# Two query chunks in turn per head group, an earlier x load, later use of GpSimd results, and more zero products in a gated mix of two attentions

## The chip, the cores and the metric

The kernel runs on one core of a Trainium2 chip, in one launch. A NeuronCore has five engines that run their own instruction queues and wait for each other by semaphores: TensorE (PE in the profile; its weight loads are PEld), VectorE (DVE), ScalarE (ACT), GpSimd (POOL) and SyncE (SP), which here only issues DMAs. The metric is the device time of one execution in microseconds, lower is better.

## The reference

Two attentions over the same input `x` (1 x 2048 x 512, bf16, 32 heads of 16), mixed by a gate for each row:

```python
g = _sigmoid((x * gate_w).sum(-1, keepdims=True))
a = _A_ref(x, A_wqkv, A_wo)        # full attention: softmax(q k^T / 4) v, then @ wo
b = _B_ref(x, B_wqkv, B_wo)        # each query sees 8 keys: positions s, s-2, ..., s-14
return g * a + (1 - g) * b
```

Part A needs 32 x 2048 x 2048 exponentials, and part B 32 x 2048 x 8.

## The kernel before

**Part A.** Queries are cut into four chunks of 512 (`QW`), heads into eight groups of four (`NG`). A pair of a chunk and a group is a period (`periods`, 32 of them, chunk by chunk: all eight groups of chunk 0, then of chunk 1, and so on). In a period the scores are made in units: 128 keys of one head against 512 queries, 64 units a period. A unit is one matmul into a slot of a PSUM ring (`qk`, tiles `ring`), one exponential (`ex`, on ScalarE, tiles `pT`) and one matmul with the values (`pv`, into `acc`). Units are taken in sets of three and two by turns, one ScalarE instruction for a set (`sets`); the ring for three and the ring for two have one buffer each. A few units of each period (`n_dve`) take another way: VectorE makes their exponential by a polynomial on the bits (`d_group`, tiles `dt`, `dg`, `pd`), so that ScalarE has fewer.

For each head group K is projected once for all 2048 keys (`k_proj`, four steps of 512 keys into `kt_all`, with a copy `kc` and a maximum `km` on VectorE; `selk` makes a scale `rowq` of the four maxima). Q is projected for each period (`q_proj`: matmuls, a mask `mg`, a scaled copy `ev` into `qt`). V is projected in blocks of heads (`v_proj`). The doubled Q and K weights `wtw` are made by `twice`, two copies each for heads 0 to 3 and for the rest. `x` comes in four tiles (`load_x`), is transposed on TensorE into PSUM (`pxt`) and copied to `xT`, half by ScalarE and half by VectorE. `warm` gives TensorE matmuls on ones before data is there.

At a period's end VectorE transposes and divides the accumulator (`po1`, `po2`, `po3`, tiles `accT`, `ott`, `oat`). When a chunk has all groups, its four row tiles are multiplied with `wo` (`a_part`, `b_part`) and leave (`dout`). For the last chunk the first three quarters of that product are made ahead, kept in the space of `kt_all`, and the rest is added at the end (`tail`).

**Part B.** For each of 16 row tiles (`b_tile`): K and V projections to a scratch in DRAM (`kv_scr`), two DMAs that bring the eight shifted neighbours (`ksh`, `vsh`), products and sums on GpSimd (`logits_half`, `av_half`, tiles `prod`, `lg`, `ob`, `obb`), a softmax in between on VectorE and ScalarE, then 16 transposes on TensorE (`fin`) and a copy on VectorE (`oe`, tile `obt`).

**The order.** No engine's order is written out by hand. Each step is an `op` with an engine, a cost, a due time `dl`, an earliest time `rel`, steps it needs (`deps`) and buffers it takes or uses (`tok`). `list_schedule` plays these on a clock of its own, engine by engine, and takes among what can start the step that is due first; `slack` adds time to a result before TensorE is thought to have it. The instructions are then issued in that order, chained on each engine, so an engine that waits for one instruction holds all behind it.

`list_schedule` also adds zero products: matmuls of zeros onto an accumulator that is in use, which change nothing in it. Where the work of the last 3.41 us (`SPAN`) falls short of a share `cover` and the list shows TensorE idle, it fills the idle time; where the lack is above `force` products, it adds one without idle time:

```python
if lack - o.zeros * ZERO > CFG["force"] * ZERO and recent and not (o.rows and rows):
    o.zeros += 1
    late = ZERO
```

The helper lines L247 (all but TensorE) and L256 (TensorE) record nearly every operation, so the profile's groups are told apart by tiles.

Of the kernel before, what the change touches and what calls it, by code (L numbers as in the profile page):

```python
# [19 lines left out]
    n_dve=(2,) * 4 + (3,) * 4 + (5,) * 18 + (6,) * 5 + (5,),  # L20
# [4 lines left out]
    force=9.0,  # L25
# [11 lines left out]
    v_slack=0.3,  # L37
    unit=0.457,
    t0=22.0,
# [5 lines left out]
H = 32  # L45
# [30 lines left out]
class Op:  # L76

    def __init__(self, eng, occ, fn, dl, deps=(), alloc=(), use=(), lat=None, rel=0.0, name="",
                 after=(), rows=False, cover=None, slack=None):
        self.eng, self.occ, self.fn, self.dl, self.rel, self.name = eng, occ, fn, dl, rel, name  # L80
        self.rows, self.zeros = rows, 0
        self.slack = (CFG["v_slack"] if eng == "dve" else 0.0) if slack is None else slack
        self.cover = cover if cover is not None else (occ if not callable(occ) else 0.0)
        self.after = [d for d in after if d is not None]
        self.deps, self.alloc = [d for d in deps if d is not None], list(alloc)
        self.lat = (occ if not callable(occ) else occ(0.0)) + LAT[eng] if lat is None else lat
        self.done = None
        for tk in list(alloc) + list(use):
            tk.ops.append(self)
# [9 lines left out]
def list_schedule(ops):  # L99
# [29 lines left out]
    while len(out) < len(ops):  # L129
# [49 lines left out]
        for s_ in succ.get(o, ()):  # L179
            left[s_] -= 1  # L180
            if left[s_] == 0:
                s_.ready = max([s_.rel] + [d.end if d.eng == s_.eng else d.done + (d.slack if s_.eng == "pe" else 0.0)
                                           for d in s_.deps]
                               + [d.t for d in s_.after])
                cand[s_.eng].append(s_)
# [4 lines left out]
def kernel(  # L190
# [94 lines left out]
    periods = [(c_, i) for c_ in range(NC) for i in range(NG)]  # L285
    NP = len(periods)
    dorder = [(t, j) for t in range(NT - 1, NT - 1 - NTD, -1) for j in range(4)]
# [31 lines left out]
    rowc = const.tile([128, 2], FP32, name="rowc")  # L319
# [3 lines left out]
    xT = const.tile([128, DC, S], BF16, name="xT")  # L323
# [11 lines left out]
    def init_dve():  # L335
        V.memset(ones_t[:], 1.0)
        V.memset(rowc[:, 0:1], 0.0)
        V.memset(rowc[:, 1:2], 1.0)
        V.memset(rowl[:], LIFT / DH)
        V.memset(magn[:], 0x7FFFFFFF)  # L340
        for j in range(4):
            V.memset(rowc[32 * j:32 * j + DH, 0:1], 1.0)
            V.memset(rowc[32 * j:32 * j + DH, 1:2], 0.0)
            V.memset(rowl[32 * j:32 * j + DH, :], 0.0)
            V.memset(magn[32 * j:32 * j + DH, :], 0xFFFFFFFF)
        V.memset(z32[:], 0.0)
        V.memset(ott2[:], 0.0)
# [10 lines left out]
    o_id = op("pool", 1.2, init_pool, -9.0)  # L358
    o_init_p = op("pool", 2.8, init_pool2, -8.0, deps=[o_id])
# [24 lines left out]
    def twice(part, h0, h1):  # L384
        def s():
            for r in range(2):
                V.tensor_copy(out=wtw[:, :, part, h0:h1, r, :],
                              in_=wraw["t"][:, part * DC:(part + 1) * DC, h0 * DH:h1 * DH].rearrange("p c (h d) -> p c h d", d=DH))
        return s
# [17 lines left out]
    o_x[0] = op("sp", 0.5, load_x(0), -9.0, alloc=[xtok[0]], lat=5.5)  # L407
    wtok = tok("vsh", 1)
    o_wk = op("sp", 0.5, load_w(1), -8.9, alloc=[wtok], lat=6.5)
    o_x[1] = op("sp", 0.5, load_x(1), -8.8, alloc=[xtok[1]], lat=7.5)  # L410
    o_x[2] = op("sp", 0.5, load_x(2), -8.7, alloc=[xtok[2]], lat=9.5)
    o_wq = op("sp", 0.5, load_w(0), -8.6, use=[wtok], lat=11.0)
    o_x[3] = op("sp", 0.5, load_x(3), -8.5, alloc=[xtok[3]], lat=12.0)
    o_wv = op("sp", 0.5, load_w(2), -8.4, lat=13.0)
    o_two = {}
    for part, o_ld, dl0 in ((1, o_wk, -6.0), (0, o_wq, -5.0)):
        o_two[part, 0] = op("dve", 0.4, twice(part, 0, 4), dl0, deps=[o_ld], use=[wtok])
        o_two[part, 1] = op("dve", 1.2, twice(part, 4, H), 4.0 - part, deps=[o_ld], use=[wtok])
# [4 lines left out]
    def warm():  # L423
        t_ = misc_ps([128, QW])
        for _ in range(3):
            mm_ct(t_, ones_t[:, 0:128], ones_t[:], True, True)
    o_warm = op("pe", 4.0, warm, -9.0, deps=[o_init_d], alloc=[tok("misc", 2)])

    o_xt = []
    for sc in range(NC):  # L430
# [13 lines left out]
        def ev(half, sc=sc, st=st):  # L444
            def s():
                dst = xT[:, 2 * half:2 * half + 2, sc * QW:(sc + 1) * QW]
                src = st["p"][:, 2 * half:2 * half + 2, :]
                if half == 0:
                    A.copy(out=dst, in_=src)
                else:  # L450
                    V.tensor_copy(out=dst, in_=src)
# [20 lines left out]
    o_selk = {}  # L472

    def k_proj(i, sc, tag, dl, rel=0.0):
# [3 lines left out]
        def part(c0, c1):  # L478
            def s():
                if c0 == 0:  # L480
                    st["pk"] = misc_ps([128, QW], tag=tag)
                for c in range(c0, c1):
                    mm_heads(st["pk"], c, 1, i, xT[:, c, sc * QW:(sc + 1) * QW], c == 0, c == DC - 1)
            return s

        def kc():
            V.tensor_scalar(out=kt_all[:, i, sc * QW:(sc + 1) * QW], in0=st["pk"][:], scalar1=rowc[:, 0:1],
# [6 lines left out]
        c = op("dve", 0.71, kc, dl - 0.8, deps=[b], use=[tk])  # L494
        return op("dve", 0.70, km, dl, deps=[b, c], use=[tk])

    def selk(i, dl):
        def s():
            V.tensor_reduce(out=kmax[:, i:i + 1], in_=kmax_all[:, i, :], axis=AX.X, op=ALU.max)
            V.scalar_tensor_tensor(out=rowq[:, i:i + 1], in0=kmax[:, i:i + 1], scalar=rowc[:, 1:2], in1=rowc[:, 0:1],  # L500
                                   op0=ALU.mult, op1=ALU.subtract)
            V.tensor_scalar(out=rowq[:, i:i + 1], in0=rowq[:, i:i + 1], scalar1=-1.0, scalar2=None, op0=ALU.mult)
        o_selk[i] = op("dve", 0.32, s, dl, deps=o_kc[i])

    for i in range(NG):
        o_kc[i] = []
        for sc in range(NC):
            if i == 0:
                o_kc[i].append(k_proj(i, sc, ("misc", "acc", "misc", "misc")[sc], -2.0 + sc))
            else:  # L510
                o_kc[i].append(k_proj(i, sc, "misc", S0[i] - 7.0 - 4.5 * (NC - 1 - sc), rel=S0[i - 1] - 6.0 if i > 1 else 10.0))
        selk(i, 2.0 if i == 0 else S0[i] - 6.0)
# [4 lines left out]
    def v_proj(h0, h1, tb, TB, tag, dl, rel=0.0):  # L517
# [4 lines left out]
        def mk(half):  # L522
            def s():
                if half == 0:
                    st["pv"] = misc_ps([128, TB, n], tag=tag)
                for tt in range(half * TB // 2, (half + 1) * TB // 2):
                    t = tb + tt
                    for c in range(DC):
                        mm(st["pv"][:, tt, :], xT[:, c, t * 128:(t + 1) * 128],
# [14 lines left out]
    v_proj(0, 4, 0, 8, "misc", 3.0)  # L544
    v_proj(0, 4, 8, 8, "misc", 4.0)
    for h0, h1, pn in ((4, 8, 1), (8, 16, 2), (16, 24, 4), (24, 32, 6)):
        TB = 512 // ((h1 - h0) * DH)
        for tb in range(0, NT, TB):
            late = tb + TB > NT - NTD
            v_proj(h0, h1, tb, TB, "misc", S0[pn] + (4.0 if late else 1.0 + tb * 1.3), rel=max(22.0, S0[pn - 1] - 4.0))  # L550


    def shift(pi):
        return cfg["shift"] if pi > NG else 0.0
# [3 lines left out]
    def q_proj(pi, tag, dl, rel=0.0):  # L558
# [6 lines left out]
        def part(c0, c1):  # L565
            def s():
# [3 lines left out]
                for c in range(c0, c1):  # L570
                    mm_heads(st["p1"], c, 0, i, xT[:, c, c_ * QW:(c_ + 1) * QW], c == 0, c == DC - 1)
# [9 lines left out]
        seq = steps(part, tk, dl - 4.0, [o_two[0, min(i, 1)], o_init_d] + o_xt[c_] + ([o_selk[i]] if pi else [o_kc[0][1]]),  # L581
# [5 lines left out]
    q_proj(0, "acc", 2.5)  # L587
# [5 lines left out]
    for sc in range(NC):  # L593
# [3 lines left out]
        def zc(sc=sc, st=st):  # L597
            st["p"] = misc_ps([1, QW])
            for c in range(DC):
                mm(st["p"][0:1, :], gw[:, c:c + 1], xT[:, c, sc * QW:(sc + 1) * QW], c == 0, c == DC - 1, tile_position=(0, 0))  # L600
# [9 lines left out]
        a = op("pe", 0.9, zc, dl, deps=[o_bw] + o_xt[sc], alloc=[tk], rel=22.0)  # L610
# [31 lines left out]
    def b_tile(t):  # L642
# [5 lines left out]
        def proj(key, off):  # L648
          def part(c0, c1):
            def s():  # L650
# [6 lines left out]
                for c in range(c0, c1):  # L657
                    mm_ct(st[key], xT[:, c, t * 128:(t + 1) * 128], bw[:, c, off * D:(off + 1) * D], c == 0, c == DC - 1)
# [169 lines left out]
    for k, us in enumerate(sets):  # L828
# [18 lines left out]
        kd = [o_kc[periods[pi][1]][t // TPC] for pi, t, j in us]  # L847
# [36 lines left out]
    def d_group(pi, gr, lo, hi):  # L884
# [44 lines left out]
        for q_, (t, j) in enumerate(gr):  # L929
            tx = tok("misc", 2)  # L930
            a = op("pe", 0.20, dq(q_), hi - 7.5 + q_, rows=True, deps=[o_q[pi], o_kc[i][t // TPC]], after=[prev or d_last[0]], alloc=[tx], use=[q_tok[pi]],
# [19 lines left out]
    for pi, (c_, i) in enumerate(periods):  # L951
# [4 lines left out]
        if i % 2 == 0:  # L956
            ott_tok[pi // 2] = tok("ott", 2)
        to = ott_tok[pi // 2]
# [6 lines left out]
        def po2(pi=pi, st=st):  # L965
# [3 lines left out]
            g0 = DH * (pi % 2)  # L969
            V.tensor_tensor(out=ott2[:, pi // 2 % 2, :, g0:g0 + DH], in0=st["a"][:, :, 0:DH], in1=rd_bc, op=ALU.mult)  # L970

        def po3(pi=pi, c_=c_, i=i):
            if c_ not in oat_tiles:
                oat_tiles[c_] = work.tile([128, NG // 2, QW], BF16, name="oat", tag="oat", bufs=2)
            V.transpose(out=oat_tiles[c_][:, i // 2, :], in_=ott2[:, pi // 2 % 2].rearrange("p b d -> p (b d)"))
        a = op("dve", 0.75, po1, E - 1.0, deps=o_pv[pi], alloc=[ta], use=[acc_tok[pi]], slack=cfg["a_slack"])
        o_ott[pi] = op("dve", 0.90, po2, E + 4.0, deps=[a], alloc=[to] if i % 2 == 0 else [], use=[ta] + ([to] if i % 2 else []))
        if i % 2:
            o_oat[pi] = op("dve", 0.74, po3, E + 6.0, deps=[o_ott[pi], o_ott[pi - 1]] + ([o_oat[pi - 2]] if pi > 1 else []),
# [6 lines left out]
    for t in range(NT):  # L986
        c_, tt = t // TPC, t % TPC
        st = {}
        last = c_ == NC - 1
        ng = NG // 2 - 1 if last else NG // 2  # L990
        E = S0[NG * c_ + 2 * ng]
        dl = E + (4.0 + 4.0 * tt if last else 10.0 + 14.0 * tt)
# [9 lines left out]
        def a_ev(st=st, t=t, tt=tt, last=last):  # L1002
            if last:
                st["fa"] = fa_view(tt)
# [25 lines left out]
        for k0 in range(0, ng, STEP):  # L1030
            k1 = min(ng, k0 + STEP)
            a = op("pe", WAVE(k1 - k0), a_part(k0, k1), dl - 4.0 + 0.3 * k0,
                   deps=[a, o_oat[NG * c_ + 2 * ng - 1], o_g, o_wo] if k0 == 0 else [a],
# [8 lines left out]
        else:  # L1042
            a = op("dve", 0.71, b_ev, dl, deps=[a, fe], use=[tk])
            tag = ("misc", "acc", "misc", "rA")[tt]
            otag = ("osb", "osb", "kvs", "kvs")[tt]
            tk, tos = tok(tag, 2 if tag == "misc" else 1), tok(otag, 2)
            E2 = S0[NP]
# [9 lines left out]
            b = op("pe", 0.26, tail, E2 + tt, deps=[o_oat[NP - 1]], alloc=[tk], use=[oat_tok[c_]])  # L1057
# [40 lines left out]
```

## Time and profile before

| | |
|---|---|
| median of the runs | 967.3 us (962.67, 967.30, 967.45) |
| profiled execution | 969.36 us, span 967.6 us |
| mean granted TensorE clock | 0.902 |
| busy: PE, DVE, ACT, POOL | 830.3, 788.3, 882.3, 741.9 us |
| exponentials of sets (ACT, `pT` from `ring`) | 761, 873.8 us |
| DMA | 47.34 MB, mean 49 GB/s |

The page gives the busy time of each engine, then the span in 40 slices: each digit is the busy share in tenths, and PEclk is the TensorE clock that was granted, in tenths of full speed. The views of waits name the engine that waited, the tile it was about to write, and what ended the wait, with the total in us, the number of times and the longest. In a timeline a row has its start, its busy time, engine, line, operation, output and input, and in brackets the idle time before it with what ended that. A view of stretches gives, for each stretch, its length, the busy time and count of PE, PEld, DVE, ACT and POOL, the granted clock, the DMA share and GB/s.

### The profile page before, as it was taken

To read this page: it belongs to the slowest core of one execution; us is meant where nothing else is said; L and a number is where in the kernel's file an instruction comes from. 1 tells how busy PE (TensorE), PEld (TensorE's weight loads), DVE (VectorE), ACT (ScalarE), POOL (GpSimd) and SP (SyncE) were. 2 spreads that over 40 slices of the span, in tenths; PEclk is the share of its full clock that TensorE was granted. 3 is DMA by queue.
4 is the path that set the end of the run, shared out by engine and by line. 5 is a ranking of instruction groups with operands and counts; after the bars stand their busy time and mean duration, and the time that the engine had idled before them with its cause. 6 is when DMAs were issued, how large, how long until landed. Compare 5 with 4: busy or idle time off the path is not lost. (4 is left out here: it accounts for less than half of the span.)

```text
span 967.6 us, 18043 instructions
## 1 busy us (share of the span) xinstructions
PE 830.3 (86%) x7361; PEld 253.5 (26%) x7361; DVE 788.3 (81%) x915; ACT 882.3 (91%) x783; POOL 741.9 (77%) x539
## 2 busy tenths in 40 slices
PE   6999989989898887788888888999798897789985
PEld 3333333232222222222222222222212222221221
DVE  5477769878879999879989989889987898988641
ACT  2799999999989998899999989899989999989996
POOL 1369688795999999999999999999999996700000
PEclk9999999899989998877898989679968979986898
DMA  8302030201311111111110311110211010000000
GB/s 262 101 2 99 1 100 1 87 12 56 99 66 56 55 56 44 55 44 46 54 49 13 104 55 54 46 44 31 69 55 50 12 50 2 1 1 1 1 1 22
DMA packets 43995, 47.34 MB, mean 49 GB/s; under 512 B 1876, under 2 KB 41348, under 8 KB 43912
## 3 DMA queue, kind: packets, MB, share of 16 engines
q1 hardware_dynamic: 43912, 46.19, 15.1%
q8 instruction: 57, 0.93, 0.4%
q14 instruction: 26, 0.21, 0.1%
HBM read 39.86 MB, written 6.33 MB: 48 GB/s over the span
## 5 line engine op out<-in xcount | busy, mean ns | idle before, releaser
L247 ACT ACTIVATE pT<-ring 128x1536 bf16<-128x1536 f32 x761 | 873.8, 1308 | 60.4 <-PE ring L256 57.4
L256 PE MATMUL ring<-qt,kt_all 32*128 32x512 bf16 x1903 | 325.5, 412 | 97.1 <-ACT pT L247 92.5
L247 POOL TENSOR_TENSOR prod<-prod 128x512 f32<-128x512 f32 (+1 forms) x208 | 314.0, 1522 | 6.3
L256 PE MATMUL acc<-pT,vp_all 128*17 128x512 bf16 (+1 forms) x1903 | 256.9, 420 | 2.2 <-DVE accT L247 1.3
L256 PEld LDWEIGHTS <-kt_all 32*128 32x128 bf16 x2048 | 104.7, 92 | 424.9 <-issue 420.3
L247 POOL TENSOR_TENSOR prod<-vsh,lg 128x512 f32<-128x512 bf16 x128 | 178.1, 1421 | 48.9 <-issue 37.8
L247 POOL TENSOR_TENSOR prod<-ksh,qb 128x512 f32<-128x512 bf16 x128 | 173.6, 1385 | 38.9 <-DMA ksh<-kv_scr 36.5
L247 DVE SCALAR_TENSOR_TENSOR dg<-dt,dg 128x1024 bf16<-128x1024 uint16 (+1 forms) x84 | 144.9, 1725 | 2.3
L247 DVE TENSOR_SCALAR dt<-misc 128x512 f32<-128x512 f32 x145 | 98.6, 687 | 50.0 <-PE misc L256 33.6
L247 DVE SCALAR_TENSOR_TENSOR pd<-dg,dt 128x1024 uint16<-128x1024 bf16 (+1 forms) x84 | 136.8, 1629 | 2.2
L247 DVE SCALAR_TENSOR_TENSOR dg<-dt 128x1024 bf16<-128x1024 uint16 (+1 forms) x84 | 121.9, 1451 | 2.7
L256 PE MATMUL acc<-ones_t,z 128*32 128x512 bf16 x292 | 110.4, 420 | 0.0
L256 PE MATMUL misc_ps<-xT,wtw 128*32 128x512 bf16 x1024 | 92.4, 419 | 3.3 <-DVE kmax_all L247 3.1
L256 PEld LDWEIGHTS <-vp_all 128*17 128x17 bf16 (+1 forms) x2048 | 48.6, 89 | 124.6 <-issue 118.6
L256 PE MATMUL misc<-qt,kt_all 32*128 32x512 bf16 x145 | 61.2, 426 | 9.0 <-DVE kvs L247 3.4
L256 PE MATMUL misc_ps<-bw,xT 128*32 128x512 bf16 x768 | 68.0, 395 | 1.1 <-DVE dt L247 0.9
L247 DVE STREAM_TRANSPOSE accT<-acc 128x512 f32<-128x512 f32 x32 | 22.7, 709 | 34.5 <-PE acc L256 34.3
L256 PEld LDWEIGHTS <-xT 128*32 128x32 bf16 (+1 forms) x1088 | 35.5, 98 | 34.3 <-issue 24.5
L256 PE MATMUL acc<-pd,vp_all 128*17 128x512 bf16 x145 | 40.3, 435 | 0.8 <-DVE pd L247 0.8
L256 PEld LDWEIGHTS <-z 128*32 128x32 bf16 x292 | 27.9, 98 | 40.1 <-issue 29.8
L256 PEld LDWEIGHTS <-wtw 128*32 128x32 bf16 x1024 | 26.4, 100 | 39.0 <-issue 22.7
L247 DVE TENSOR_SCALAR kt_all<-misc_ps,rowc 128x512 bf16<-128x512 f32 x32 | 25.7, 804 | 11.9 <-PE misc_ps L256 11.7
(68 smaller groups left out, 468.1 us busy)
## 6 DMA issues: line engine op xcount, KB each, us to landing
ksh<-kv_scr SPq DMA_DIRECT2D x16, 1024.0 KB, 6.0
vsh<-kv_scr SPq DMA_DIRECT2D x16, 1024.0 KB, 5.5
kv_scr<-kvs SPq DMA_DIRECT2D x16, 256.0 KB, 2.1
xld<-in_A_x_dram SPq DMA_DIRECT2D x4, 512.0 KB, 8.0
out_dram<-osb SPq DMA_DIRECT2D x16, 128.0 KB, 1.7
bw<-in_B_wqkv_dram SPq DMA_DIRECT2D x1, 1536.0 KB
wraw<-in_A_wqkv_dram SPq DMA_DIRECT2D x2, 512.0 KB, 8.2
wv<-in_A_wqkv_dram SPq DMA_DIRECT2D x1, 512.0 KB, 9.0
```

What stands on the lines that cost most here:

```text
L247: return chain_on(key, f(*a, **k))
L256: return chain(nc.tensor.matmul(out, lhsT=lhsT, rhs=rhs, start=start, stop=stop, **kw))
```

## The change

The periods run over pairs of chunks: group 0 of chunk 0, group 0 of chunk 1, group 1 of chunk 0, and so on, then the same for chunks 2 and 3. Each head group's K and V are therefore first needed two periods after those of the group ahead, and two chunks end together. Both of the last two chunks now have their product made ahead in part. `n_dve` is given anew (142 units for VectorE, before 145).

The fourth tile of `x` is loaded ahead of the Q weights; `xT` is two tiles, one for each copying engine; the K copies of group 0 go to ScalarE; the doubled weights, but for the K weights of heads 0 to 3, are made by GpSimd; `warm` has 32 matmuls and not 12; the first V projections and the K projections of group 1 come after the start; `rowq` needs one instruction less.

In the list a result of GpSimd counts 4 us later for any engine that takes it up (`g_slack`), and `force` goes from 9 to 1. The start of the exponentials that the due times are reckoned from (`t0`) goes from 22.0 to 18.5.

```diff
-    n_dve=(2,) * 4 + (3,) * 4 + (5,) * 18 + (6,) * 5 + (5,),
+    n_dve=(3,) * 2 + (4,) * 14 + (5,) * 16,
-    force=9.0,
+    force=1.0,
+    g_slack=4.0,
-    t0=22.0,
+    t0=18.5,
...
-        self.slack = (CFG["v_slack"] if eng == "dve" else 0.0) if slack is None else slack
+        self.slack = {"dve": CFG["v_slack"], "pool": CFG["g_slack"]}.get(eng, 0.0) if slack is None else slack
...
-                s_.ready = max([s_.rel] + [d.end if d.eng == s_.eng else d.done + (d.slack if s_.eng == "pe" else 0.0)
+                s_.ready = max([s_.rel] + [d.end if d.eng == s_.eng else d.done + (d.slack if s_.eng == "pe" or d.eng == "pool" else 0.0)
...
-    periods = [(c_, i) for c_ in range(NC) for i in range(NG)]
+    periods = [(2 * cp + s, i) for cp in range(NC // 2) for i in range(NG) for s in range(2)]
...
-    xT = const.tile([128, DC, S], BF16, name="xT")
+    xTs = [const.tile([128, 2, S], BF16, name=f"xT{h}") for h in range(2)]
...
+            E_ = V if part == 1 and h0 == 0 else G
             for r in range(2):
-                V.tensor_copy(out=wtw[:, :, part, h0:h1, r, :],
+                E_.tensor_copy(out=wtw[:, :, part, h0:h1, r, :],
...
-    o_wq = op("sp", 0.5, load_w(0), -8.6, use=[wtok], lat=11.0)
-    o_x[3] = op("sp", 0.5, load_x(3), -8.5, alloc=[xtok[3]], lat=12.0)
+    o_x[3] = op("sp", 0.5, load_x(3), -8.6, alloc=[xtok[3]], lat=9.2)
+    o_wq = op("sp", 0.5, load_w(0), -8.5, use=[wtok], lat=10.2)
...
-        for _ in range(3):
+        for _ in range(8):
             mm_ct(t_, ones_t[:, 0:128], ones_t[:], True, True)
...
         def kc():
+            if i == 0:
+                A.activation(out=kt_all[:, i, sc * QW:(sc + 1) * QW], in_=st["pk"][:], func=ACT.Identity, scale=rowc[:, 0:1],
+                             bias=rowc[:, 1:2])
+                return
...
-                o_kc[i].append(k_proj(i, sc, "misc", S0[i] - 7.0 - 4.5 * (NC - 1 - sc), rel=S0[i - 1] - 6.0 if i > 1 else 10.0))
-        selk(i, 2.0 if i == 0 else S0[i] - 6.0)
+                o_kc[i].append(k_proj(i, sc, "misc", S0[2 * i] - 16.0 - 9.0 * (NC - 1 - sc), rel=max(T0 + 1.0, S0[2 * i] - 60.0)))
+        selk(i, 2.0 if i == 0 else S0[2 * i] - 15.0)
...
-    v_proj(0, 4, 0, 8, "misc", 3.0)
-    v_proj(0, 4, 8, 8, "misc", 4.0)
-    for h0, h1, pn in ((4, 8, 1), (8, 16, 2), (16, 24, 4), (24, 32, 6)):
+    v_proj(0, 4, 0, 8, "acc", T0 + 2.0, rel=T0 - 2.0)
+    v_proj(0, 4, 8, 8, "misc", T0 + 3.0, rel=T0 - 2.0)
+    for h0, h1, pn in ((4, 8, 2), (8, 16, 4), (16, 24, 8), (24, 32, 12)):
...
-        last = c_ == NC - 1
+        last = c_ >= NC - 2
```

## The prediction

> **What bounds the kernel now.** I read the page first, for which engine has no spare time, then the waits, then stretches of the trace with their granted clock, then single moments. The page:
>
> ```profile
> PE 830.3 (86%) x7361; PEld 253.5 (26%) x7361; DVE 788.3 (81%) x915; ACT 882.3 (91%) x783; POOL 741.9 (77%) x539
> ...
> ACT  2799999999989998899999989899989999989996
> ...
> PEclk9999999899989998877898989679968979986898
> ```
>
> ScalarE is full from the third of the 40 slices to the end. Its work is 761 exponentials, one per set, and no edit makes one cheaper. So the time is: the start up to the first exponential, 761 sets, what delays a set, and the tail. The waits say what delays one (us in total, times, longest):
>
> ```profile
> PE ring L256 <- ACT pT L247: 92.5, 281, 1.3
> ACT pT L247 <- PE ring L256: 57.4, 76, 9.4
> ...
> POOL prod L247 <- DMA ksh<-kv_scr: 36.5, 1, 36.5
> ...
> PE misc_ps L789 <- POOL obb L247: 4.3, 1, 4.3
> ```
>
> ScalarE waits 57.4 us for scores; 9.4 of them lie before the first exponential, 48 later. Where those 48 fall is seen in stretches (length, busy time and count by engine, clock, DMA):
>
> ```profile
> 30.00:176.00 146.00, 134.39 (x1448) 47.37 (x1440) 104.88 (x156) 143.39 (x130) 105.83 (x87) 1.00 0.18 55
> 273.00:367.00 94.00, 79.60 (x765) 25.44 (x758) 88.15 (x92) 93.23 (x84) 92.20 (x64) 1.00 0.19 59
> 405.30:422.40 17.10, 13.98 (x81) 2.79 (x83) 10.48 (x12) 11.22 (x10) 16.63 (x13) 0.50 0.19 62
> 879.80:896.80 17.00, 17.00 (x78) 2.73 (x76) 11.94 (x13) 14.95 (x14) 0.00 (x0) 0.50 0.00 1
> ```
>
> At full clock ScalarE is 98 to 99% busy; at half clock 66 and 88%. The trace holds 21 half-clock stretches after the start, 181 us together, each a multiple of 3.41 us. I cut the full-clock time into windows of 3.41 us and counted how long the array streamed in each (a 512-column pass as 0.213 us): all 16 windows under 45% were followed by half clock, 5 of 39 between 45 and 55%, none of 159 above. So thin TensorE work, not only standing still, brings the half clock here.
>
> Last, the start and one stall:
>
> ```profile
> 1.89 2.13 POOL L247 MEMSET vp_all<- 128x480 bf16 x1
> ...
> 11.09 0.69 DVE L247 COPY xT<-pxt 128x1024 bf16<-128x1024 bf16 x1 [2.32 <-ACT xT L247]
> ...
> 27.03 0.81 DVE L247 TENSOR_SCALAR qt<-misc_ps,rowq,rowl 128x512 bf16<-128x512 f32 x1
> ...
> 28.33 3.90 ACT L247 ACTIVATE pT<-ring 128x1536 bf16<-128x1536 f32 x3 [9.40 <-PE ring L256]
> ```
>
> ```profile
> 408.42 0.62 PE L789 MATMUL misc_ps<-ident,obb 128*32 128x128 bf16 x16 [4.28 <-POOL obb L247]
> ...
> 409.68 1.02 ACT L247 ACTIVATE pT<-ring 128x1024 bf16<-128x1024 f32 x1 [3.72 <-PE ring L256]
> ```
>
> ScalarE starts at 28.33, behind VectorE, which works almost without a gap from 14.4 to 27.8. And TensorE once stood 4.28 us before the transposes of a GpSimd result, score matmuls queued behind them; ScalarE lost 3.72.
>
> **The start.** From 14.36 on VectorE's row holds, before the first exponential, five K copies (0.80 each, 4.0), two copies of doubled weights (0.35 and 1.15) and one reduce for head group 1 (0.68) that are gone from there in the new order, and one small rowq step (0.15): 6.3 us, which gives 22.0. The other way is the new chain. One 512 KB load lands every 1.5 us (transposes released at 5.11 and 8.12, the K weight copy at 6.59), so x tile 3 lands near 11.1 instead of 12.6 and the Q weights near 12.6 instead of 11.1. From there: transposes 1.07 per tile, ScalarE's x copy 1.01, VectorE's 0.69 still behind it (the order keeps that wait), the reduce 0.68, ScalarE's K copy behind the reduce (512 columns: between 0.55, half the 1.01 of 1024, and VectorE's 0.80), K matmuls 1.05 per half, the mask 0.75, maxima and rowq 0.4, qt 0.81, scores 0.4: 20.0 with TensorE at full clock from 6 us, 22.5 when it stays at half to 12.7 as before (32 K matmuls took 3.27 there, against 1.05 for 16 later). The 32 warming matmuls instead of 12 decide that; they end near 4.9, before x lands at 5.1, so they cost nothing. I take 21.0: **-7.3** (-5.8 to -8.3). What had been done before the start now stands between the first score matmuls: half of the V projection (64 matmuls took 2.73, so 1.4), K matmuls of group 1 and B projections. Covered, it costs nothing; uncovered up to 3.5; **+1.5**, about the V half, since only two score rings are ahead there.
>
> **GpSimd copies of weights.** Two copies of 256 columns, then four of 1792, no row of which is on GpSimd. Nearest rows: the plain memset 0.55 for 544 (1.0 ns a column), the products 1.42 for 512 (2.8), the strided memset 2.13 for 480 (4.4). TensorE's first K matmul of group 1 stands behind set 3 and waits for the second large copy; behind it on TensorE are all later scores. The Q weights land at 12.6; the K copies are done at 16.7, 24.0 or 30.8 by the three prices, and TensorE is there at about 24.4. Cost 0, 0 or 6.4; I take 0, by the products, which read bf16 with the same inner runs of 16. GpSimd's own first product waited for ksh until about 38, so it loses nothing.
>
> **Head groups in turn.** Units on ScalarE rise from 1903 to 1906, so at 28.33 to 958.8 for 1903, 0.49 each: **+1.4** for three. VectorE loses three units of 0.69 and 2.8 (its dg and pd rows, 403.6 us for 145), 10 us, off the path. The rest is where K and V projections stand: spread over sixteen periods, not eight. I counted TensorE's 512-column passes between score matmuls, per set, in sixths of the sets. Before: 3.86, 3.69, 3.27, 3.40, 3.41, 3.33, with half clock for 0, 12, 41, 55, 44, 27 us (the stretches' clocks). After: 3.68, 3.57, 3.65, 3.50, 3.31, 3.52. Read off the first pairs, that is some 13, 27, 17, 34, 40, 32 us: 163 instead of 181. A half-clock microsecond costs between 0.10 (half-clock stretches against 1.15 us a set at full clock, the stalled one corrected) and 0.30 (all 55 us by which 761 sets exceed 1.15 each, over 181). 18 at 0.14: **-2.5** (0 to -5.4).
>
> **GpSimd results later.** The order puts the sixteen transpose groups behind sets 71, 120, ... 334 (tile 6), ... 692. At 1.22 us a set from 21.0 each stands 14 us or more behind the time when GpSimd finished that tile before (tile 6: 428 against 408.4). The stall goes: **-3.7** (0 if GpSimd, which itself waits longer for softmax, slips as far; it ended at 842, so its slip alone costs nothing). Next late there is the score ring itself, 0.2 us.
>
> **Zero products everywhere.** 316 instead of 292; 43 of the new ones the list puts where it shows no idle stretch. At 0.213 that is 9.2 us put ahead of ready matmuls; TensorE waited 92.5 us for ScalarE's rings, which covers most. 0 to 9.2, taken at a quarter, since TensorE streams two thirds of full-clock time: **+2.0**.
>
> **Outputs and queues.** Two chunks' outputs come together, as many matmuls and copies as before, 0. On SP x tile 3 passes the Q weights (counted), and eight output DMAs stand last instead of four, four of them due a period earlier. Tail, 958.8 to 967.6, unchanged: 0, at worst +2.3 (the four last issues took 2.31).
>
> Sum: -7.3 + 1.5 + 1.4 - 2.5 - 3.7 + 2.0 = -8.6. The profiled execution took 969.4 with a span of 967.6; it becomes 960.8. The median of the runs is 967.3, so 958.7.
>
> **Rivals.**
> *Half clock spreads (slower).* The first 300 us are nearly free of it now, and exactly they get thinner; single windows decide, not means: stretches of three sets in which TensorE's work fills under half the time number 0 in sets 52 to 102 before and 9 after. Against: over the whole order they fall from 84 to 76. If the first two sixths become like the third (41 each) and the rest stays, half clock grows by 70 instead of shrinking: at 0.20, the middle of the two prices, 958.7 + 2.5 + 14 = 975. It decides from some 55 us of growth, where 972.1 is reached.
>
> *The GpSimd copies hold TensorE.* At 4.4 ns a column: 958.7 + 6.4 = 965. For: GpSimd's strided row. Against: its products. [...]
>
> *The zero products buy nothing.* If only standing still dropped the clock, the 43 would be pure TensorE time: 958.7 + 2.5 + 7.2 = 968. Against it stand the 21 falls: the longest TensorE stop after the start is 4.28 us, and the falls follow thin windows. [...]
>
> *The clock mostly holds.* If zero products and evenness cut half clock to 60 us, 121 at 0.20 go: 958.7 + 2.5 - 24 = 937. Against: the passes per set stay under 3.6 in four sixths.
>
> **How the numbers follow.** Forecast 0.54, half clock spreads 0.13, copies 0.14, zero products 0.07, clock holds 0.12. A measurement of this kernel tells about 0.5% from no change, so the borders are 962.5 and 972.1. The forecast's bounds add up to 951 at the good end and, halfway to all the bad ends, to 967; a quarter of it lies above 962.5. Faster: 0.40 + 0.12 + part of the copies' case, 0.10: 0.62. Slower: 0.13 and 0.03 from the forecast's worst sums: 0.16. Same: 0.22. The range leaves out half of the last rival and of the first: 943 to 975.
>
> **What would show it.** Right: first exponential at 20 to 22.5; no wait of TensorE for a GpSimd result above 1 us; half clock 140 to 185 us, more of it before 330 us and less behind; 763 exponentials of the same durations; tail near 8.8. Wrong: TensorE waiting for the doubled weights near 25 us; the clock of the first two stretches under 0.93; sets at full clock slower than 1.15 us, which would be the forced zero products.

## The result, and the profile after

| | before | after |
|---|---|---|
| median of the runs | 967.06 us (960.29 to 972.00) | 960.77 us (954.15 to 967.79) |
| profiled execution, its span | 969.36, 967.6 us | 963.95, 961.8 us |
| granted TensorE clock there | 0.902 | 0.917 |
| first exponential, last one's end | 28.33, 958.8 us | 21.57, 953.0 us |
| stretch between them (the row) | 930.5 us | 931.4 us |
| half clock in the row | 181 us in 21 falls | 154 us in 20 falls |
| tail | 8.8 us | 8.8 us |

Both medians are of 20 runs, taken beside each other. The ratio after to before is 0.9927, 95% interval 0.9906 to 0.9948: faster by 0.7%, 6.3 us in the medians and 5.4 us in the profiled pair. Of the 5.4, the start gives 6.8 and the row takes 0.9 back; 0.4 is time outside the profiled span. In the table of experiments the medians, the ratios and the means of half clock leave out six executions, of e3, e4, e6 and e7, that lay over 1.5% above their kernel's fastest.

The page of the kernel after, busy times and two rows of the 40 slices:

```profile
PE 828.1 (86%) x7405; PEld 254.6 (26%) x7405; DVE 769.1 (80%) x887; ACT 886.2 (92%) x789; POOL 750.9 (78%) x545
...
ACT  4899999999998899999988989979999999999995
...
PEclk9998999999998799989977989978999898999677
```

ScalarE now works from the end of the first slice on, and is still the full engine. Of the clock's slices 14 are below 9, where 18 were; the first of them is the fourth now (the eighth before), and the last three are low.

The waits (us in total, times, longest):

```profile
PE ring L257 <- ACT pT L248: 96.1, 287, 1.0
...
ACT pT L248 <- PE ring L257: 53.0, 73, 2.6
...
POOL prod L248 <- DMA ksh<-kv_scr: 21.4, 1, 21.4
...
POOL wtw L248 <- DMA wraw<-in_A_wqkv_dram: 8.9, 1, 8.9
```

ScalarE waited 57.4 us for scores before and waits 53.0 now. But 9.4 of the 57.4 lay ahead of the first exponential and 1.7 of the 53.0 do: inside the row it went from 48.0 to 51.3. All of ScalarE's idle time in the row, whatever the reason, is the same in both executions, 53.5 us: the row is 0.9 us longer because ScalarE works 0.9 us more in it. No wait of TensorE for GpSimd's `obb` is left in this view (4.3 us before). GpSimd's first products wait 21.4 us for `ksh`, not 36.5, behind the weight copies that it now makes first.

Two stretches (length, busy time and count by engine, clock, DMA share, GB/s):

```profile
30.00:176.00 146.00, 127.68 (x1273) 41.98 (x1265) 109.64 (x142) 140.41 (x127) 107.54 (x81) 0.96 0.17 53
313.80:324.00 10.20, 9.92 (x72) 2.09 (x70) 7.03 (x8) 7.55 (x7) 9.89 (x10) 0.50 0.01 2
```

The first is the same 146 us that ran at clock 1.00 with ScalarE busy 143.39 before. It has three windows of half clock now, and ScalarE is busy 140.41. The second is one of the half-clock stretches: ScalarE 7.55 of 10.20, 74%, as before between 66 and 88%.

The start, in the timeline:

```profile
10.88 0.78 ACT L248 ACTIVATE kt_all<-misc_ps,rowc 128x512 bf16<-128x512 f32 x1 [0.70 <-DVE kmax_all L248]
...
12.99 7.24 POOL L248 COPY wtw<-wraw 128x256 bf16<-128x256 bf16 x6 [8.94 <-DMA wraw<-in_A_wqkv_dram]
...
19.28 0.95 DVE L248 SCALAR_TENSOR_TENSOR rowq<-kmax,rowc 128x1 f32<-128x1 f32 x1
20.27 0.81 DVE L248 TENSOR_SCALAR qt<-misc_ps,rowq,rowl 128x512 bf16<-128x512 f32 x1
...
21.57 3.71 ACT L248 ACTIVATE pT<-ring 128x1536 bf16<-128x1536 f32 x3 [1.70 <-PE ring L257]
```

K copies on ScalarE take 0.78 us. The six weight copies of GpSimd, 7680 columns, take 7.24 us, 0.94 ns a column. `qt` is made at 20.27, not 27.03, and the exponentials begin at 21.57.

### The profile page after: what moved, and what is told of

It is laid out like the page before. It is cut to its first block, busy times and chain, and to the rows that moved or that the text cites. A ratio compares the mean times of both kernels' runs of the same rounds, so it can differ in the third digit from the quotient of the medians.

```text
span 961.8 us, 18102 instructions
## 1 busy us (share of the span) xinstructions
PE 828.1 (86%) x7405; PEld 254.6 (26%) x7405; DVE 769.1 (80%) x887; ACT 886.2 (92%) x789; POOL 750.9 (78%) x545
## 4 chain that ended last, share of the span: by engine, by line
ACT 32%; PE 27%; DVE 22%; issue 16%; DMA 2%; ACTq 0%; SPq 0%; DVEq 0%
ACT pT L248 31%; PE acc L257 9%; PE ring L257 9%; DVE dg L248 8%; PE misc_ps L257 7%; DVE pd L248 4%; DVE dt L248 2%; PE misc L257 2%; DVE ott L248 1%; DVE accT L248 1%; DVE lg L248 1%; DMA z_scr<-zrow 1%; DMA xld<-in_A_x_dram 1%; DVE qt L248 1%; DVE rr L248 1%
## 5 line engine op out<-in xcount | busy, mean ns | idle before, releaser
L248 ACT ACTIVATE pT<-ring 128x1536 bf16<-128x1536 f32 x763 | 875.4, 1308 | 55.2 <-PE ring L257 53.0
L257 PE MATMUL ring<-qt,kt_all 32*128 32x512 bf16 x1906 | 319.3, 407 | 102.5 <-ACT pT L248 96.1
L248 POOL TENSOR_TENSOR prod<-prod 128x512 f32<-128x512 f32 (+1 forms) x208 | 305.3, 1480 | 6.3
L257 PE MATMUL acc<-pT,vp_all 128*17 128x512 bf16 (+1 forms) x1906 | 253.0, 413 | 7.8 <-DVE accT L248 6.5
L248 POOL TENSOR_TENSOR prod<-ksh,qb 128x512 f32<-128x512 bf16 x128 | 185.2, 1477 | 47.5 <-DMA ksh<-kv_scr 21.4
L248 POOL TENSOR_TENSOR prod<-vsh,lg 128x512 f32<-128x512 bf16 x128 | 181.7, 1450 | 38.3 <-issue 24.7
L248 DVE SCALAR_TENSOR_TENSOR dg<-dt,dg 128x1024 bf16<-128x1024 uint16 (+1 forms) x80 | 137.2, 1715 | 2.1
L248 DVE SCALAR_TENSOR_TENSOR pd<-dg,dt 128x1024 uint16<-128x1024 bf16 (+1 forms) x80 | 133.4, 1668 | 2.0
L257 PE MATMUL acc<-ones_t,z 128*32 128x512 bf16 x316 | 114.3, 415 | 0.0
L257 PE MATMUL misc<-qt,kt_all 32*128 32x512 bf16 x142 | 58.4, 411 | 6.9 <-DVE kvs L248 2.2
L248 DVE TENSOR_SCALAR misc_ps<-misc_ps,magn 128x512 uint32<-128x512 uint32 x32 | 23.9, 747 | 11.4 <-PE misc_ps L257 11.4
```

Source lines behind the costliest of these rows:

```text
L248: return chain_on(key, f(*a, **k))
L257: return chain(nc.tensor.matmul(out, lhsT=lhsT, rhs=rhs, start=start, stop=stop, **kw))
```

## Experiments

Each kernel was timed beside the kernel before on the same chip. "Half" is the mean over the kernel's executions, worked out as 2 x (1 - granted clock) x span, because every stretch of the clock in the traces of both kernels (46 before, 42 after) is at 1.0 or at 0.5. In 69 executions of the kernel before it is 162 us on average, and 190 in the profiled one; in the 20 of the kernel after, 156. "Row" and "zeros" (zero products) are of the profiled execution. "Idle" is ScalarE's idle time in the row where the clock had been full for 1.5 us, read instruction by instruction.

| | edit | ratio, 95% interval | median | row | idle | half | zeros |
|---|---|---|---|---|---|---|---|
| before | | 1 | | 930.5 | 10.3 | 162 | 292 |
| after | whole change | 0.9927 [0.9906, 0.9948] | 960.8 | 931.4 | 11.8 | 156 | 316 |
| e1 | before + new start | 1.0085 [1.0052, 1.0118] | 976.5 | 943.6 | 17.9 | 190 | 304 |
| e5 | e1 with `t0` 19.6 | 0.9987 [0.9967, 1.0006] | 968.0 | 937.5 | 21.8 | 149 | 314 |
| e9 | before + new start + slack | 1.0019 [0.9993, 1.0046] | 969.5 | 943.6 | 11.0 | 198 | 302 |
| e10 | before + new start + `force` 1 | 0.9924 [0.9898, 0.9950] | 960.3 | 926.5 | 15.2 | 160 | 318 |
| e11 | before + `force` 1 | 1.0061 [1.0040, 1.0082] | 974.2 | 935.2 | 14.9 | 156 | 357 |
| e2 | after, periods chunk by chunk | 0.9916 [0.9887, 0.9946] | 958.4 | 932.5 | 15.1 | 152 | 327 |
| e3 | after, `force` 9 | 0.9978 [0.9957, 0.9998] | 965.1 | 932.8 | 13.2 | 177 | 275 |
| e7 | after, no slack | 0.9934 [0.9901, 0.9967] | 962.1 | 932.7 | 18.2 | 148 | 320 |
| e6 | after, another list | 0.9924 [0.9893, 0.9954] | 960.6 | 929.9 | 14.2 | 137 | 346 |
| e4 | after, no zero products | 1.0287 [1.0245, 1.0329] | 996.6 | 974.4 | 6.1 | 424 | 0 |
| e8 | after, `cover` 0.76 | 0.9900 [0.9875, 0.9925] | 957.5 | 923.3 | 12.2 | 129 | 446 |
| e12 | after, `cover` 0.85 | 0.9941 [0.9923, 0.9960] | 962.6 | 930.8 | 21.4 | 99 | 630 |

In every kernel with the new start the first exponential stands between 21.0 and 22.0 us; in e11 it stands at 28.4, as before.

### The start alone

e1 is the kernel before with the new start (loads of `x`, two `xT` tiles, K copies on ScalarE, weight copies on GpSimd, 32 warming matmuls, V and K work behind the start), its order of periods, `force` 9 and no slack:

```diff
-    t0=22.0,
+    t0=18.8,
...
-    xT = const.tile([128, DC, S], BF16, name="xT")
+    xTs = [const.tile([128, 2, S], BF16, name=f"xT{h}") for h in range(2)]
...
+            E_ = V if part == 1 and h0 == 0 else G
...
-    v_proj(0, 4, 0, 8, "misc", 3.0)
-    v_proj(0, 4, 8, 8, "misc", 4.0)
+    v_proj(0, 4, 0, 8, "acc", T0 + 2.0, rel=T0 - 2.0)
+    v_proj(0, 4, 8, 8, "misc", T0 + 3.0, rel=T0 - 2.0)
```

> The kernel before with the new start alone (x tile 3 ahead of the Q weights, xT in two tiles, the K copies of group 0 on ScalarE, doubled weights on GpSimd, 32 warming matmuls, V projections and K of group 1 after the start; the list's start t0 18.8, since with 18.5 this mix of steps has no order). Periods chunk by chunk, force 9, no slack for GpSimd. Theory S, the gain is the start: first exponential near 21.6 us as in the changed kernel, 6.8 earlier than 28.3; the time 967 - 6.8 + 0 to 1.5 = 960 to 962, as good as the whole change. Rival O, the order of the periods brings the gain and an earlier start is given back at the next waits: first exponential early, but 965 to 967.

The exponentials began at 21.6, 6.7 us earlier, and the kernel was slower: the row took 943.6 us, 13.1 more than before. To see whether that lay in the edits or in the order that the list makes of them, e5 moves one number of the list and changes no step of the kernel's own work (the list then adds 314 zero products, not 304):

```diff
-    t0=18.8,
+    t0=19.6,
```

> The new start alone once more (the same steps as in the first run of it, which took 976.5), with the list's start t0 at 19.6 instead of 18.8: another order of the same steps, 314 zero products instead of 304. Theory L, the lists scatter: how the steps happen to fall sets waits and thin windows anew each time, and the time is anywhere from 958 to 972. Rival W, the earlier start without the GpSimd slack and without forced zero products is given back whatever the order: 973 to 979 again, with the first exponential still at 21.6.

The same steps in another order were 0.0098 better, some 9.5 us, with intervals that don't meet. So another order, with the zero products that it takes, is worth about 1% here, more than the whole change. In neither list did the start's gain stay. In e5 it was not the clock: half clock is below that of before (157 us in the profiled row against 181), and the row is 7 us longer, because ScalarE idles 21.8 us at full clock and not 10.3. In e1 both were larger. Between the profiled executions of e1 and e5 the clock is what differs: e1's row is 6.1 us longer although ScalarE idles 3.9 us less there at full clock, with 191 us of half clock in it against 157.

### GpSimd's slack

e9 adds the slack to the start; e7 takes it from the kernel after:

```diff
+    g_slack=4.0,
-    t0=18.8,
+    t0=18.0,
...
+        self.slack = {"dve": CFG["v_slack"], "pool": CFG["g_slack"]}.get(eng, 0.0) if slack is None else slack
...
-                s_.ready = max([s_.rel] + [d.end if d.eng == s_.eng else d.done + (d.slack if s_.eng == "pe" else 0.0)
+                s_.ready = max([s_.rel] + [d.end if d.eng == s_.eng else d.done + (d.slack if s_.eng == "pe" or d.eng == "pool" else 0.0)
```

> The new start and the 4 us for GpSimd results, without the new order of periods and with force 9 (t0 18.0, 302 zero products). The start alone took 968 and 976.5 in two orders: the first exponential came 7 us earlier, but ScalarE's row had 9 to 12 us more of idle stretches over 0.6 us at full clock, among them 3 and 9 us behind GpSimd results. Theory G, an earlier ScalarE row meets GpSimd results that are not earlier, and the 4 us keep them out of the way: waits for GpSimd results under 2 us in sum, full-clock idle stretches over 0.6 us back to 4 to 6 us, 960 to 963. Rival F, the zero products kept the gain: 966 to 972 here.

```diff
-    g_slack=4.0,
+    g_slack=0.0,
```

> The changed kernel with GpSimd results counted as ready at once (g_slack 0; 320 zero products). Theory S: stalls of TensorE for a GpSimd result come back, one or two of 3 to 4 us as in the kernel before, and each costs ScalarE 3 us or more: 964 to 968. Theory L: a difference of that size is within what another order does; then the page shows no stall above 1 us and the time is anywhere from 954 to 970.

e9 has 1.0019, below e1 (1.0085) and, within the intervals, not to be told from e5 (0.9987); TensorE still waits for `obb` there, 3.2 us. e7, without the slack, is as fast as the kernel after, within what the two intervals tell, and its view of waits has no wait of TensorE for `obb`. Other lists with the slack have them: 3.0 us in e2, 2.6 in e3, 9.0 in e12. So the stall and the slack do not go together in these lists, and no worth of the slack shows on either side: e9's 0.0066 below e1 is less than the 0.0098 that another order alone gave.

### force

```diff
-    force=9.0,
+    force=1.0,
```

e10 puts this on the start (with `t0` 18.0), e11 on the kernel before, and e3 takes it back (1.0 to 9.0) in the kernel after.

> The new start and force 1, without the new order of periods and without the 4 us (t0 18.0, 318 zero products). Theory G: waits for GpSimd results of 3 to 9 us stay, 965 to 970. Rival F, the forced zero products keep the gain: 959 to 963 although the waits stay.

> The kernel before with force 1 alone (357 zero products instead of 292). Taking force 1 out of the changed kernel cost 5 us, of 961. If that is the zero products' worth, they give as much here: 961 to 965, with 20 to 40 us less half clock than the 160 that this kernel has on average. If it was the other order of the steps, this lies anywhere from 960 to 974, and half clock and time do not go together.

> The changed kernel with force 9, so that zero products stand only where the list shows an idle stretch (275 instead of 316). Theory S, the forced ones cost about 2 us of TensorE time on the path and buy about as much clock: 958 to 962, half clock up by 0 to 30 us from 154. Rival C, they hold the clock: half clock over 190 us and 966 to 970. Rival N, they buy nothing and cost all their TensorE time: half clock as with them and 952 to 955.

e10 has the whole gain of the change, without the order by pairs and without the slack. The waits of e5 and e10 show what does not separate them. First e5:

```profile
ACT pT L247 <- PE ring L256: 55.4, 69, 4.2
...
PE misc_ps L798 <- POOL obb L247: 5.2, 4, 2.7
...
DVE mx L247 <- POOL lg L247: 4.0, 4, 2.3
```

and e10:

```profile
ACT pT L247 <- PE ring L256: 41.4, 59, 3.6
...
DVE mx L247 <- POOL lg L247: 6.7, 6, 3.6
PE misc_ps L798 <- POOL obb L247: 5.4, 3, 3.5
```

TensorE waits for GpSimd as long in both, and VectorE longer in e10; ScalarE waits 14.0 us less for scores there, and the row is 11.0 us shorter. Nor is it the number of zero products (314 and 318), or the half clock on average (149 and 160 us). In the two profiled executions the half clock of the rows does differ, 157 and 137 us; but ScalarE's idle time at full clock alone is 6.6 of the 11.0 us shorter (21.8 and 15.2). What changed there is the order of the list, and between e1 and e5 a new order was worth as much. In the kernel after, `force` changed the number as well: e3 has 275 zero products, 21 us more half clock on average and a ratio 0.0051 higher, 4.9 us, with intervals that do not meet; but its list is another order as well. And with the old start `force` 1 made the kernel slower, e11, with 65 zero products more than before.

The lists with the new start and `force` 1 (after, e2, e6, e7, e10) all lie between 0.9916 and 0.9934, the four with the new start and `force` 9 (e1, e3, e5, e9) between 0.9978 and 1.0085. That is a pattern of nine lists. A part of it is the clock: e1, e3 and e9 have 177 to 198 us of half clock on average, the five with `force` 1 have 137 to 160. At 0.13 to 0.24 us for each, prices that are worked out below, this is 3 to 10 us of the 5 to 15 by which the three lie behind the kernel after. It does not hold for e5, with 149. And why `force` 9 should bring it is not shown: e1, e5 and e9 have nearly as many zero products, 302 to 314, as e10 with 318.

### The order of the periods

```diff
-    periods = [(2 * cp + s, i) for cp in range(NC // 2) for i in range(NG) for s in range(2)]
+    periods = [(c_, i) for c_ in range(NC) for i in range(NG)]
```

With it the due times of K and V, `n_dve` (145 units) and the ends of the chunks are those of before; start, slack and `force` 1 stay (`t0` 18.3).

> The changed kernel with the periods chunk by chunk again (with the due times, the units for VectorE and the last chunk's products of before; t0 18.3); the start, the 4 us for GpSimd results and force 1 stay. Theory S: the order of the periods is worth what the sum gave it, three units less (-1.4) and the clock's -2.5 lost, so 960.8 - 1.4 + 2.5 = 962, half clock 160 to 185 us, nearly all of it after 330 us as in the kernel before. Rival O: without the new order half clock grows over 200 us and the time is 966 or more. Second rival: the old order is the better one, since its first 300 us stay at full clock, 955 to 958.

0.9916 against 0.9927, half clock 152 and 156 us: taking the head groups in turn for two chunks bought nothing that this measurement can tell.

### Another list of the kernel after

```diff
-    unit=0.457,
+    unit=0.4573,
```

The cost that the list reckons for a unit moves by 0.3 ns, so that the order changes, and with it the number of zero products, but nothing else.

> The changed kernel with the list's unit at 0.4573 instead of 0.457 us, which moves every due time by less than 0.1% and nothing else in what is done: another order of the same steps (346 zero products instead of 316). Theory L: the time lies elsewhere within 954 to 970, with half clock and stalls in other places. Rival W, the gain belongs to the steps: 958 to 963.

0.9924 against 0.9927, with 346 zero products instead of 316. The gain of the kernel after is not one lucky order, though one other list is a small sample beside the 1% between e1 and e5.

### The dose of zero products

e4 leaves out all zero products, which change no value; e8 and e12 ask for more.

```diff
-            lack = COVER * SPAN - sum(x[1] for x in recent) - o.cover
+            lack = 0.0
```

> The changed kernel without any zero product (316 left out). If thin windows bring the half clock: TensorE's work falls from about 3.55 to 3.1 passes a set, below every sixth of either trace, where 3.3 stood with 27 to 44 us of half clock in about 155; so at least 60 us in each sixth, 360 in all against 154, and at 0.14 to 0.24 us lost for each that is 29 to 50 us: 990 to 1010. If only a standing TensorE brought it: no stop of 3.4 us comes from leaving the products out, the clock stays as it is, and the path gets shorter by what they cost: 950 to 960.

The page of e4:

```profile
PE 877.5 (87%) x7089; PEld 225.7 (22%) x7089; DVE 749.3 (75%) x887; ACT 894.5 (89%) x789; POOL 743.9 (74%) x545
...
PEclk9987897979688878675896788766568555977555
```

and two neighbouring stretches:

```profile
68.00:86.60 18.60, 16.67 (x197) 5.81 (x196) 12.81 (x22) 18.39 (x18) 8.90 (x8) 1.00 0.22 71
86.60:103.70 17.10, 16.59 (x102) 2.98 (x102) 11.10 (x11) 13.75 (x12) 16.86 (x12) 0.50 0.22 63
```

TensorE is busier than ever, 877.5 us, because it runs at half clock for 462 us of the row in this execution, where a score matmul takes 470 ns on average and 407 in the kernel after (1006.9 us, the longest of its runs, granted 0.764; the other five were granted 0.779 to 0.801). Up to 86.60 ScalarE was busy 18.39 of 18.60 us; then, with TensorE at half clock and busy for 16.59 of 17.10 us, 13.75 of 17.10. TensorE's longest gap between instructions in the row is under 1.5 us in this trace, and the clock fell 36 times: no window stood idle. Of the full-clock windows of 3.41 us that streamed under 45%, all 22 were followed by half clock, of those between 45 and 55% 14 of 29, above that none of 99. In the kernel after, 18 of 19 windows under 45%, 2 of 9 up to 50% and none of 200 above were followed by half clock.

e4 also prices both sides. Against the kernel after the ratio is 0.0360 higher, 35 us, for 269 us more half clock: 0.13 us each, net of what the zero products cost. Their own cost is small, by an estimate: where the clock is full, two sets follow each other in 2.303 us here and in 2.316 in the kernel after, 0.013 more, which over some 310 pairs is 4 us for all 316 zero products, if the whole difference is theirs.

The 0.13 is no constant. Executions of one and the same kernel differ in half clock too, and there a straight line through time against half clock gives another price: 0.24 us for each in the 20 executions of the kernel after (133 to 183 us of half clock, correlation 0.94), but only 0.04 to 0.10 in the three groups of executions of the kernel before. So the price differs from list to list; what sets it is not shown.

```diff
-    cover=0.68,
+    cover=0.76,
```

> The changed kernel with zero products aimed at 0.76 of the last 3.41 us instead of 0.68: 446 instead of 316. Leaving all 316 out cost 36 us and brought 300 us more half clock, 0.12 us for each. If the rest of the half clock (154 us) goes the same way, 130 more products take away 60 to 120 us of it, worth 7 to 14 us, and cost TensorE 130 x 0.213 = 28 us, of which a quarter on the path, 7: 953 to 961. Rival: TensorE becomes what holds ScalarE at full clock, too, sets at full clock take 1.19 us instead of 1.16: 965 to 980.

```profile
PE 822.9 (86%) x7535; PEld 259.0 (27%) x7535; DVE 767.5 (80%) x887; ACT 885.7 (93%) x789; POOL 756.0 (79%) x545
...
ACT  4999999999999999999988999998988989989995
...
PEclk9999999999899999999988989997988878999777
```

The clock is at 9 in 19 of the first 20 slices, and ScalarE in all of these but the first. 446 zero products, 129 us half clock, 923.3 us for the row, 0.9900: the fastest of all the kernels run, faster than both, though its interval overlaps that of the kernel after. The half clock fell by 27 us, where 60 to 120 had been expected. By 0.13 us each these are 3.5 us; the ratio's 0.0027 are 2.6.

```diff
-    cover=0.68,
+    cover=0.85,
```

> The changed kernel with zero products aimed at 0.85 instead of 0.68 of the last 3.41 us: 630 instead of 316. So far 0, 275, 316 and 446 products gave 997, 966, 961 and 957.5 us with some 430, 181, 156 and 129 us of half clock. If each further product keeps buying clock: half clock under 80 us and 948 to 955. Rival, at 446 the gain has run out: TensorE's own time holds the scores, sets at full clock take over 1.18 us (1.16 now), and the time is 962 to 975.

630 zero products bring half clock down to 99 us and the time up again, to 0.9941: 30 us less half clock should have given 3.9 us, and 4.0 were lost against e8, with intervals that just touch. ScalarE idles 21.4 us at full clock, 9.2 more than in e8, and pairs of sets follow each other there in 2.352 us, 2.326 in e8. Its longest wait is not among the 21.4, because the clock falls within it, at 808.87. In the timeline:

```profile
810.44 0.62 PE L803 MATMUL misc_ps<-ident,obb 128*32 128x128 bf16 x16 [5.35 <-POOL obb L248]
...
811.71 3.79 ACT L248 ACTIVATE pT<-ring 128x1536 bf16<-128x1536 f32 x3 [5.71 <-PE ring L257]
```

TensorE stood 5.35 us before the transposes of a GpSimd result, and ScalarE lost 5.71 behind it: the stall of before, in another place and in spite of the slack. Whether the zero products or merely this list put it there is not separated.

## Why the prediction was right, and where not

**The result** is 960.8 where 958.7 was forecast, inside the range and faster by over 0.5%.

**The start** was right in its place and its size: -6.8 for -7.3. The first exponential came at 21.57, where 21.0 was taken. Full clock held from 6.63 us on, K copies took 0.78, inside the bounds of 0.55 and 0.80, and x tile 3 and the Q weights changed places as reckoned. The 21.0 was a choice between 20.0 and 22.5 and not a sum, so the half microsecond between has no one cause: the term had 0.4 for the maxima and `rowq`, and `rowq` alone took 0.95, told below; but e3, in which it took 0.22, began no earlier, at 21.80.

**Work moved behind the start, +1.5.** The first sixth of the sets took 1.195 us a set instead of 1.170, 3.2 us for 127 sets, with 10 us of half clock that were not there before. At 0.13 to 0.24 each those are 1.3 to 2.4, so up to 1.9 is left. e10 and e5, with the same work moved behind the start and no half clock in their first sixth, took 1.169 and 1.217 us a set there: what the moved work costs hangs on the list, and no run gives it a price of its own.

**Three units more, +1.4.** 763 exponentials, 875.4 us busy for 873.8: +1.6.

**The clock, -2.5.** In the profiled pair the row's half clock fell from 181 to 154 us, where 163 was read off. By sixths of the sets it was 10, 21, 10, 39, 32, 41 us, for 13, 27, 17, 34, 40, 32: thinner TensorE work in the first two, more of it at the third, as the passes per set had said. But the base was wrong. The profiled execution of before had 190 us in its whole span, the average of 69 has 162; the kernel after averages 156. What the change is worth in half clock is 6 us, not 18, some 0.8 us by the price of e4. The price taken, 0.14, is the one between e4 and the kernel after; the 0.24 among executions of the kernel after lies inside the bounds of 0.10 to 0.30 too.

**GpSimd results later, -3.7.** The sign of it came: no such wait is left, and every transpose stands behind its tile. The gain did not. ScalarE's waits for scores inside the row rose from 48.0 to 51.3 us without the stall: its idle times beside half clock went from 43.2 only to 41.7, and those of 0.3 to 1.2 us at full clock rose from 6.4 to 9.7. e7, without the slack, has no such stall either and is as fast, and e10 has the whole gain with 5.4 us of TensorE waiting for `obb`. The failing step was to price a stall at its own length and to put "0.2 us" next in line, when the order that removes it makes other waits. That these are the price of the slack itself was not shown.

**Zero products, +2.0.** The term priced their TensorE time alone; the clock that they hold stands in the passes per set of the clock term. The price was too high: by the estimate from e4, 4 us for all 316, the 43 forced ones cost 0.5. Taken with the clock they are a gain, not a loss: e4 puts what all of them save, net, at 35 us, and with the forced ones taken out e3 is 4.9 us longer, though in another order. The sign that was named for it, sets at full clock slower than 1.15 us, could not tell: pairs of sets follow each other in 2.316 us there, 1.158 a set, but in 2.310 before, 1.155.

So the row's terms, -1.3 together, came to +0.9, with the stall's gain and the clock's taken too large on one side and the zero products' cost on the other. That these errors cancel in part is luck, and the sum stood by the start.

**The rivals.** Half clock spreads: the first two sixths did rise, from 14 to 31 us, but the total fell; e1 and e9 show the rival in other lists, 190 and 198 us and slower or no faster. GpSimd copies: 0.94 ns a column, below the lowest of the three prices, and TensorE does not wait for them; one small VectorE instruction, 0.95 us long, ended with the last of them, as told below. Zero products buy nothing: refuted by e4. The clock mostly holds: no kernel came to its 60 us; e12 came nearest with 99, and without the gain that this rival gave it.

**What stays open** is why, among nine lists with the new start, the 6.8 us stay in the five that have `force` 1 and not in the four that have 9. More half clock is a part of the answer for three of the four, but not for e5. That two orders of the same steps lie 1% apart is measured; which property of an order ScalarE's short waits follow is not. The sum came out well because the start's gain stayed, and that it would stay was assumed in it, not worked out: e1 and e5 show that it need not.

## What to carry to other kernels

A gain at the start of a kernel whose order a program makes is a change of the whole order: time it in a second list before you credit or blame the edit, for two lists of the same steps lay 1% apart here. Before a term is taken from the difference to one profiled execution, look at how that execution lies among the runs: 190 us of half clock in the profile stood against 162 on average. Work that only keeps TensorE streaming can be worth its cost, and its dose has to be tried: here 316 zero products saved 35 us net for an estimated 4, the best of the doses was 446, and at 630 ScalarE idled 9.2 us more at full clock than at 446 and the ratio rose from 0.9900 to 0.9941.

## What the runs showed of the hardware

**A small VectorE instruction that ended with a GpSimd copy.** The first `rowq`, 128 x 1 out of `kmax` and `rowc`, took 0.22 us in the kernel before. In the kernel after it took 0.95 and ended at 20.23 us, and GpSimd's last weight copy ends at 12.99 + 7.24 = 20.23. In e2:

```profile
12.50 7.23 POOL L248 COPY wtw<-wraw 128x256 bf16<-128x256 bf16 x6 [8.45 <-DMA wraw<-in_A_wqkv_dram]
...
18.76 0.98 DVE L248 SCALAR_TENSOR_TENSOR rowq<-kmax,rowc 128x1 f32<-128x1 f32 x1
```

18.76 + 0.98 = 19.74 against 12.50 + 7.23 = 19.73. In e3 it comes later:

```profile
12.61 7.23 POOL L248 COPY wtw<-wraw 128x256 bf16<-128x256 bf16 x6 [8.57 <-DMA wraw<-in_A_wqkv_dram]
...
20.25 0.22 DVE L248 SCALAR_TENSOR_TENSOR rowq<-kmax,rowc 128x1 f32<-128x1 f32 x1
```

GpSimd has ended at 19.84, and it takes 0.22. In the kernel after `rowq` held up `qt`, which comes next, by 0.7 us. Beside the same copies the mask took 0.76 us and the reduces of K 0.68 and 0.69, for 0.75 and 0.68 in the kernel before. Why `rowq` and the copy ended together was not shown.

**How half clock ends.** In e4 and in the kernel after, TensorE streamed more in the windows at which half clock ended than in many that full clock outlasted: no full-clock window above 55% (e4) or 50% (the kernel after) was followed by half clock. Of the half-clock windows of e4 that streamed under 80%, 1 of 57 was followed by full clock, of those above 85% 30 of 50; in the kernel after 2 of 10 and 16 of 22. A fall lasted 13 us on average in e4 (462 us in 36 falls), 8 in the kernel after (154 in 20).

**The same kernel's half clock varies by execution.** The kernel before was granted between 0.902 and 0.931 on average over an execution, 190 to 133 us of half clock. One execution would not have told this kernel's clock.
